# Unfolding products read PSUM, the first batch in a new block order with loads in halves, and a layout that knows the shared port

## The chip, the cores and the metric

One Trainium2 chip, one core of it. The metric is the device time of one execution in microseconds (us), median over several executions; lower is better. The engines are TensorE (PE; its weight loads are PEld), VectorE (DVE), ScalarE (ACT), GpSimd (POOL) and SyncE (SP), which issues all DMAs here.

## What is computed

Two stages over 8 batches, 8 heads, 576 positions, head size 64, all in float32. Stage 1 is attention in a sliding window; stage 2 takes its output as x and runs four small causal attentions ("experts") that a gate mixes, two per position.

```python
scores = scale * (q @ k.T)
mask = (rel >= 0) & (rel < 64)
attn = softmax(where(mask, scores, -1e9)) @ v
x = attn.transpose(0, 2, 1, 3).reshape(B, S, H * D)

logits = x @ w_gate
w = softmax of the two largest logits of a position
for e in range(4):
    q, k, v = x @ wq[e], x @ wk[e], x @ wv[e]
    a = softmax(where(causal, scale * (q @ k.T), -1e9))
    out += w[e] * (a @ v @ wo[e])
```

## The kernel before

The work is written as small functions and put in order by a planner. Class `Plan` records every engine call with a due time `at` and a cost; `order` is a list scheduler: on each engine it takes the ready operation with the smallest `at` whose buffers are free, and the calls are then issued in that order, which is fixed from there on. Waits on the chip come from data and buffers alone; each engine works its own queue from the front.

**Stage 1** works in 36 units `u` of 8 blocks. A block is 64 queries of one pair of heads `p` (four pairs make a batch, nine blocks a pair), so a batch is 36 blocks or 4.5 units, taken pair by pair.
- `s1_qk` (line 338): 32 small products into two PSUM banks `s1` (tag "s", 5 banks); ACT and DVE bring them to SBUF tile `sm`, folded, so that a row holds only the 64 scores of its window (ACT copies the earlier part, POOL writes it for a head's first block, DVE lays the own block over it); then DVE takes the row maximum, POOL subtracts it, ACT takes the exponential, DVE sums and inverts, POOL scales. The last lines load the next pair's q and k.
- `s1_t` (line 373): PE turns `sm` in four transposes into a PSUM bank `t1` (tag "t", 3 banks); ACT copies it to SBUF tile `f` (`ft`, 2 buffers); from `f` the folded rows are unfolded into `pt`: two triangle products on DVE (`pt<-ft,tri`) and two `affine_select` on POOL (`pt<-ft`).
- `s1_av` (line 393): 32 products with v into a bank `o1` (tag "t"); ACT writes the result rounded as `XH`, DVE the remainder as `XL`.

**Stage 2** of a batch takes `XH`, `XL` of all four pairs: `s2_v` (values and gate, four tiles of 128 positions and one tail), `proj` (`s2_k`, `s2_q`, columns in halves by `HALVES`), scores `s2_mm`, softmax `s2_soft`, `s2_t`, `s2_av_mm`, `s2_o`. The weights are loaded by `load_weight` and split into two parts by ACT and DVE (`split_weights`). Due times come from the tables `POS`, `BPOS` and `WPOS`.

Loads at the start, in SP's order: q and k of pair 0, of pair 1, v of pair 0, q and k of pair 2, v of pair 1, then weights, each tile whole; q, k and v have three buffers each, so pair p+3 is loaded where pair p is done with.

Of the kernel before, what the change touches and what calls it, by code (L numbers as in the profile page):

```python
# [8 lines left out]
F32 = mybir.dt.float32  # L9
# [18 lines left out]
FIXED = (1.0, 15.5)  # L28
WPOS = [-0.776, -0.284, -0.071, 1.269]
CPOS = 0.202  # L30
BPOS = ((0.044, 0.7), (0.088, 0.667), (0.08, 0.3, 0.12), (-0.413, -0.1))
PARTS = ((0, 5), (5, 9))
HALVES = ((0, 320), (320, 256))


class Plan:
# [64 lines left out]
    def link(self):  # L101
        seen, tiles = {}, {}
        for op in self.ops:
            deps, spare = {}, set()
            for x, w in op["use"]:
                if x.space not in (PSUM, bass.MemoryType.SB):
                    continue
                t = x.tensor.name
                box = self.box(x)
                bank = x.space == PSUM  # L110
                if t not in tiles:
                    tiles[t] = dict(first=op, ops=[], tag=x.tensor.tag, bufs=x.tensor.tag_meta.bufs, bank=bank)
                if not any(op is o for o in tiles[t]["ops"]):
                    tiles[t]["ops"].append(op)
                for other, b, ww in seen.setdefault(t, []):
                    if other is op:
                        continue
                    hit = box[0] < b[1] and b[0] < box[1] and box[2] < b[3] and b[2] < box[3]
                    if hit and (w or ww) or bank and other["engine"] != op["engine"]:
                        deps[other["n"]] = deps.get(other["n"], True) and (w and not bank)  # L120
                seen[t].append((op, box, w))
            op["deps"] = deps
        for t in tiles.values():
            t["left"] = len(t["ops"])
            for op in t["ops"]:
                op.setdefault("tiles", []).append(t)
        for t in tiles.values():
            first = t["first"]
            if t["bank"]:
                later = [o for o in t["ops"] if o["engine"] != "P"]  # L130
                for o in later:
                    for d, buffer_only in o["deps"].items():
                        if buffer_only and d < first["n"]:
                            first["deps"].setdefault(d, True)
                    for u in o["tiles"]:
                        if not u["bank"] and u["first"]["n"] > first["n"]:
                            u["first"] = first
                            for v in u["ops"]:
                                if v["n"] > first["n"]:
                                    v["deps"].setdefault(first["n"], True)  # L140
        for t in tiles.values():
            t["first"].setdefault("takes", []).append(t)
        return tiles

    def order(self):
# [16 lines left out]
        mode = None  # L162
        events = [0.0]
        ends = []
        done, now = [], 0.0
        while len(done) < len(ops):
# [18 lines left out]
            for e in "PAVGS":  # L185
# [25 lines left out]
                clock[e] = now + max(20, cost - self.OVERLAP[e])  # L211
# [7 lines left out]
        return done  # L219

    def place(self, op, mode):
        return op["at"]

    def issue(self):
        for op in self.order():
# [17 lines left out]
def window_attention_moe_attention(ctx: ExitStack, tc: tile.TileContext, qT, kT, vW,  # L243
# [9 lines left out]
    pairs = {}  # L253

    def load_pair(p):
        q_t = load.tile([128, S], F32, tag="q", bufs=3, name=f"q{p}")
        nc.sync.dma_start(q_t, qT[p])
        k_t = load.tile([128, S + 64], F32, tag="k", bufs=3, name=f"k{p}")
        nc.sync.dma_start(k_t, kT[p])
        pairs[p] = [q_t, k_t, None]  # L260

    def load_v(p):
        v_t = load.tile([128, 2, BLK, 64], F32, tag="v", bufs=3, name=f"v{p}")
        nc.sync.dma_start(v_t, vW[p].rearrange("r (h b c) -> r h b c", h=2, b=BLK))
        pairs[p][2] = v_t

# [4 lines left out]
    load_pair(0)  # L271
    load_pair(1)
    load_v(0)
    load_pair(2)
    load_v(1)


    own = const.tile([128, 64], mybir.dt.uint8, name="own")
# [51 lines left out]
    SM, PT1 = {}, {}  # L330
    XH, XL, XT = {}, {}, {}

    def tiles(u):
        for i in range(8):
            t = 8 * u + i
            yield i % 2, i // 2, t // BLK, t % BLK

    def s1_qk(u):

        banks = [psum.tile([128, 4, 128], F32, tag="s", bufs=5, name=f"s1_{u}_{x}") for x in range(2)]  # L340
        with nc.block():
            for x, j, p, b in tiles(u):
                c0 = 64 * int(b == 0)
                for h in range(2):
                    r, o = slice(64 * h, 64 * h + 64), 64 * (h ^ x)
                    nc.tensor.matmul(banks[x][o:o + 64, j, c0:], lhsT=pairs[p][0][r, 64 * b:64 * b + 64],
                                     rhs=pairs[p][1][r, 64 * b + c0:64 * b + 128], start=True, stop=True)
        sm = SM[u] = work.tile([128, 2, 4, 64], F32, tag="sm1", bufs=3, name=f"sm1_{u}")
        st = work.tile([128, 3, 8], F32, tag="st1", bufs=3, name=f"st1_{u}")
        first = {(x, j) for x, j, p, b in tiles(u) if b == 0}  # L350
# [9 lines left out]
            nc.vector.copy_predicated(sm[:, x], own[:, None, :].to_broadcast([128, 4, 64]), banks[x][:, :, 64:128])  # L360
        flat = sm.rearrange("r x j c -> r (x j) c")
        nc.vector.tensor_reduce(st[:, 0], flat, axis=AX.X, op=OP.max, negate=True)
        nc.gpsimd.tensor_tensor(flat, flat, st[:, 0, :, None].to_broadcast([128, 8, 64]), op=OP.add)
        nc.scalar.activation(flat, flat, AF.Exp, scale=0.125)
        nc.vector.tensor_reduce(st[:, 1], flat, axis=AX.X, op=OP.add)
        nc.vector.tensor_scalar_add(st[:, 1], st[:, 1], 1e-9)
        nc.vector.reciprocal(st[:, 2], st[:, 1])
        nc.gpsimd.tensor_tensor(flat, flat, st[:, 2, :, None].to_broadcast([128, 8, 64]), op=OP.mult)
        for x, j, p, b in tiles(u):
            if b == BLK - 1 and p + 3 < NB * NP:  # L370
                load_pair(p + 3)

    def s1_t(u):

# [3 lines left out]
            for i in range(4):  # L378
                nc.tensor.transpose(ps[:, i], sm[:, 128 * i:128 * i + 128], ident)
        t = PT1[u] = work.tile([128, 4, 2, 128], F32, tag="pt1", bufs=2, name=f"pt1_{u}")  # L380
        f = work.tile([128, 4, 128], F32, tag="ft", bufs=2, name=f"ft_{u}")
        nc.scalar.activation(f, ps, AF.Copy)
        for e in range(2):
            r = slice(64 * e, 64 * e + 64)
            nc.vector.tensor_mul(t[0:64, :, e], f[r],
                                 tri[r].rearrange("r a c -> r (a c)")[:, None, :].to_broadcast([64, 4, 128]))
            nc.gpsimd.affine_select(out=t[64:128, :, e].rearrange("r i (a c) -> r i a c", a=2),
                                    in_=f[r].rearrange("r i (a c) -> r i a c", a=2), pattern=[[0, 4], [0, 2], [1, 64]],
                                    base=0, channel_multiplier=-1, compare_op=OP.is_ge, fill=0.0)

    freed = []

    def s1_av(u):
# [11 lines left out]
        while i < 8:  # L405
            b9, k = divmod(8 * u + i, NP * BLK)
            n = min(8 - i, NP * BLK - k)
            if k == 0:
                XH[b9] = work.tile([128, NP * S], F32R, tag="xh", name=f"xh{b9}")
                XL[b9] = work.tile([128, NP * S], F32R, tag="xl", name=f"xl{b9}")  # L410
            c = slice(64 * k, 64 * (k + n))
            src = o[:, i:i + n].rearrange("r t c -> r (t c)")
            nc.scalar.activation(XH[b9][:, c], src, AF.Copy)
            nc.vector.tensor_sub(XL[b9][:, c], src, XH[b9][:, c])
            if k + n == NP * BLK:
                if b9 % 2 == 0:
                    for x in range(2):
# [5 lines left out]
        while freed and freed[0] + 3 in pairs:  # L423
            load_v(freed.pop(0) + 3)

# [119 lines left out]
                nc.vector.tensor_copy(G2[h][64:128, :, 7:9], src[64 * h:64 * h + 64, 0])  # L545

    def proj(b, name, pr, half):
        c0, n = HALVES[half]
# [194 lines left out]
    def s2_o(b, j):  # L743
        ps = psum.tile([128, DM], F32, tag="s", bufs=5, name=f"ops_{b}_{j}")
        with nc.block():
            for pr in range(2):
                y0 = y_col(b, 2 * j) if j < 4 else 512
                yh, yl = (y[pr][:, y0:y0 + 128] for y in (YH, YL))
                three(ps, yh, yl, whi["o"][:, pr], wlo["o"][:, pr], pr == 0, pr == 1)
        t = work.tile([128, DM], F32, tag="out", bufs=2, name=f"out_{b}_{j}")  # L750
        nc.vector.tensor_copy(t, ps)
        if j < 4:
            nc.sync.dma_start(out[b, 128 * j:128 * j + 128], t)
# [71 lines left out]
    todo.append((CPOS, stage2_constants, ()))  # L825
    todo.append((WPOS[2] + 1e-3, clear_pt2, ()))
    for i in range(4):
        load_weight(i)
        if i == 0:
            load_v(2)  # L830
    todo.sort(key=lambda x: x[0])
    for t, f, args in todo:
        nc.at = t
# [57 lines left out]
```

## Time and profile before

| | us |
|---|---|
| median of 3 runs | 513.28 (512.98 to 515.19) |
| profiled execution, its own time | 516.96 |
| its span, first to last instruction | 515.2 |
| TensorE busy | 476.6 (93%) |
| VectorE busy | 371.2 (72%) |
| ScalarE busy | 299.0 (58%) |
| GpSimd busy | 262.7 (51%) |
| DMA moved | 51.29 MB, mean 100 GB/s |

The profile is of one execution; its time is 3.7 us above the median of the runs. All rows name line 227, the planner's recording of a call, so groups are told by their tiles. [...]

### The profile page before, as it was taken

The numbers are of one execution on the slowest core, as the hardware profiler recorded it, in microseconds if no ns is written. First come the engines' busy times: TensorE is split into PE (matmuls) and PEld (weight loads), VectorE is DVE, ScalarE is ACT, GpSimd is POOL, SyncE is SP. The second block draws the span as 40 slices with busy tenths as digits, with TensorE's granted clock in tenths as the row PEclk, the third lists the DMA queues.
The fourth block names the chain that finished last, engine by engine and source line by source line (L and its number), as shares of the span: only waits on it lengthen the run. The fifth ranks groups of instructions, "written<-read, shape, count | busy, mean of one in ns | idle before, by whom it ended". The sixth has DMA issues, their size and how long they took to land.

```text
span 515.2 us, 14666 instructions
## 1 busy us (share of the span) xinstructions
PE 476.6 (93%) x5672; PEld 417.5 (81%) x5672; DVE 371.2 (72%) x1178; ACT 299.0 (58%) x929; POOL 262.7 (51%) x439
## 2 busy tenths in 40 slices
PE   4558989999999999999999999999999999999986
PEld 3447977888988888888888888888888888898774
DVE  5878778987676877878686777878677775644713
ACT  2534355766557475656657565665756575656651
POOL 5748727583566545383565536384465534422130
PEclk9966998999999999999999999999999999999979
DMA  8745432131552323241543223241341000201103
GB/s 297 292 124 197 136 115 78 68 95 48 186 156 77 98 87 96 74 135 46 160 155 103 73 91 116 63 146 46 115 147 60 1 22 22 63 1 43 42 1 103
DMA packets 20630, 51.29 MB, mean 100 GB/s; under 512 B 2768, under 2 KB 3280, under 8 KB 20560
## 3 DMA queue, kind: packets, MB, share of 16 engines
q1 hardware_dynamic: 20560, 50.35, 29.8%
q8 instruction: 45, 0.74, 0.6%
q14 instruction: 25, 0.20, 0.1%
HBM read 40.90 MB, written 9.44 MB: 98 GB/s over the span
## 4 chain that ended last, share of the span: by engine, by line
PE 66%; DVE 13%; POOL 12%; ACT 3%; issue 3%; DMA 1%; SPq 0%; POOLq 0%; DVEq 0%
PE s L227 14%; PE o L227 12%; PE t L227 11%; PE ops L227 10%; PE v2ps L227 8%; PE qps L227 7%; PE kps L227 5%; POOL p L227 5%; DVE st L227 4%; POOL sm L227 4%; POOL pt L227 3%; DVE g L227 2%; DVE p L227 1%; DMA k<-in_kT_dram 1%; DVE sm L227 1%
## 5 line engine op out<-in xcount | busy, mean ns | idle before, releaser
L227 POOL TENSOR_TENSOR sm<-sm,st 128x512 f32<-128x512 f32 x72 | 77.6, 1078 | 72.3 <-DVE st L227 52.7
L227 PE MATMUL o<-pt,v 128*64 128x64 f32 (+3 forms) x2048 | 95.3, 250 | 9.1 <-DVE pt L227 3.9
L227 PEld LDWEIGHTS o<-pt,v 128*64 128x64 f32 x2048 | 85.6, 144 | 20.1 <-POOL pt L227 9.5
L227 ACT ACTIVATE p<-p,r 128x192 f32<-128x192 f32 (+3 forms) x128 | 77.4, 607 | 31.9 <-DVE r L227 31.5
L227 POOL TENSOR_SCALAR_AFFINE_SELECT pt<-ft 64x512 f32<-64x512 f32 x72 | 64.4, 894 | 61.5 <-ACT ft L227 58.3
L227 POOL TENSOR_SCALAR p<-p,r 128x192 f32<-128x192 f32 (+3 forms) x128 | 77.9, 625 | 31.9 <-DVE r L227 14.8
L227 ACT ACTIVATE pt<-t 128x512 f32<-128x512 f32 (+2 forms) x192 | 69.5, 388 | 22.1 <-PE t L227 20.1
L227 DVE CUSTOM_DVE_ANT_0 p<-s,causal 128x320 f32<-128x320 f32 (+3 forms) x160 | 68.2, 470 | 7.1 <-PE s L227 6.6
L227 DVE TENSOR_TENSOR pt<-ft,tri 64x512 f32<-64x512 f32 x72 | 62.6, 869 | 4.8 <-ACT ft L227 3.5
L227 DVE TENSOR_REDUCE st<-sm 128x8 f32<-128x512 f32 x72 | 49.1, 684 | 17.0 <-ACT sm L227 15.8
L227 PE MATMUL t<-ident,p 128*128 128x128 f32 x384 | 59.2, 283 | 1.6 <-POOL p L227 1.5
L227 PE MATMUL s<-kt,qt 64*128 64x256 f32 (+2 forms) x480 | 55.0, 334 | 2.7 <-DVE sm L227 1.1
L227 PE MATMUL s<-k,q 64*64 64x128 f32 (+1 forms) x1152 | 45.5, 298 | 7.9 <-DMA k<-in_kT_dram 7.9
L227 PEld LDWEIGHTS t<-ident,p 128*128 128x128 f32 x384 | 44.3, 144 | 10.4 <-issue 2.7
L227 PEld LDWEIGHTS s<-k,q 64*64 64x64 f32 x1152 | 36.5, 151 | 14.7 <-issue 6.1
L227 DVE COPY_PREDICATED sm<-own,s 128x256 f32<-128x256 uint8 x72 | 30.5, 444 | 24.4 <-POOL sm L227 13.3
L227 PEld LDWEIGHTS s<-kt,qt 64*128 64x128 f32 x480 | 36.2, 185 | 13.0 <-issue 3.8
L227 PE MATMUL qps<-xh,wqhi 128*128 128x320 f32 (+1 forms) x128 | 40.7, 318 | 0.0
L227 PE MATMUL kps<-xh,wkhi 128*128 128x320 f32 (+1 forms) x128 | 39.6, 310 | 0.0
L227 ACT ACTIVATE sm<-sm 128x512 f32<-128x512 f32 x36 | 22.7, 630 | 28.2 <-POOL sm L227 27.8
L227 PE MATMUL v2ps<-wvhi,xh 128*128 128x260 f32 x128 | 38.8, 303 | 0.0
L227 PE MATMUL qps<-xl,wqhi 128*128 128x320 f32 (+1 forms) x128 | 37.8, 295 | 0.0
(105 smaller groups left out, 1044.3 us busy)
## 6 DMA issues: line engine op xcount, KB each, us to landing
v<-in_vW_dram SPq DMA_DIRECT2D x32, 576.0 KB, 4.1
k<-in_kT_dram SPq DMA_DIRECT2D x32, 320.0 KB, 3.9
q<-in_qT_dram SPq DMA_DIRECT2D x32, 288.0 KB, 3.0
out_dram<-out SPq DMA_DIRECT2D x32, 256.0 KB, 2.1
out_dram<-out SPq DMA_DIRECT2D x8, 128.0 KB, 2.3
pt<-in_wv_dram SPq DMA_DIRECT2D x1, 512.0 KB, 8.9
pt<-in_wk_dram SPq DMA_DIRECT2D x1, 512.0 KB, 8.8
pt<-in_wq_dram SPq DMA_DIRECT2D x1, 512.0 KB, 8.5
```

The lines of the kernel that those rows point to most:

```text
L227: call(*args, **kw)
```

## The change

1. Unfolding (`s1_t`): the triangle product reads the PSUM bank instead of the SBUF copy, in all units (`UNFOLD = (2, 2)`); POOL's selects still read the copy, which now has one buffer.
2. First batch: q and k of all four pairs are loaded, first columns 0 to 255, then the rest; `ORDER` takes blocks 0 to 3 of every pair first, then blocks 4 to 8; q, k and v have four buffers and k loses its 64 columns of zeros; `HALVES` of batch 0 is 256 and 320 columns. Units below `EARLY = 5` fold the subtraction of the maximum into eight exponentials of 64 columns with a bias, in place of POOL's subtraction. The splits into `XH`, `XL` follow the new block order.
3. Planner: operations that hold the port that VectorE and GpSimd share are charged for each other; all operations of a tile with several buffers wait for the tile's first one; due times of the weight loads; in the last batch the even output tiles take the buffers of `sm`. `AFFINITY = 0.0` changes nothing.

```diff
-HALVES = ((0, 320), (320, 256))
+HALVES = (((0, 256), (256, 320)), ((0, 320), (320, 256)))
...
+        sb = [x for x in outs + ins if x.space != PSUM]
+        op["port"] = engine == "G" or engine == "V" and (
+            len([x for x in sb if x in ins]) > 1 or len(sb) == len(outs + ins) and name in (
+                "tensor_copy", "tensor_scalar", "tensor_scalar_add"))
...
+                if best["port"]:
+                    cost += max(0.0, port - now)
+                    port = now + cost
...
-        q_t = load.tile([128, S], F32, tag="q", bufs=3, name=f"q{p}")
-        nc.sync.dma_start(q_t, qT[p])
-        k_t = load.tile([128, S + 64], F32, tag="k", bufs=3, name=f"k{p}")
-        nc.sync.dma_start(k_t, kT[p])
+        q_t = load.tile([128, S], F32, tag="q", bufs=4, name=f"q{p}")
+        k_t = load.tile([128, S], F32, tag="k", bufs=4, name=f"k{p}")
         pairs[p] = [q_t, k_t, None]
+        if p >= NP:
+            load_part(p, 0, S)
...
+    for p in range(NP):
+        load_part(p, 0, 256)
+    for p0 in (0, 2):
+        for p in (p0, p0 + 1):
+            load_part(p, 256, S)
+        for p in (p0, p0 + 1):
+            load_v(p)
...
+    ORDER = [(p, b) for p0 in (0, 2) for p in (p0, p0 + 1) for b in range(4)]
+    ORDER += [(p, b) for p in range(NP) for b in range(4, BLK)]
+    ORDER += [(p, b) for p in range(NP, NB * NP) for b in range(BLK)]
...
-        nc.gpsimd.tensor_tensor(flat, flat, st[:, 0, :, None].to_broadcast([128, 8, 64]), op=OP.add)
-        nc.scalar.activation(flat, flat, AF.Exp, scale=0.125)
+        if u < EARLY:
+            nc.vector.tensor_scalar(st[:, 0], st[:, 0], 0.125, None, op0=OP.mult)
+            for i in range(8):
+                nc.scalar.activation(flat[:, i], flat[:, i], AF.Exp, bias=st[:, 0, i:i + 1], scale=0.125)
+        else:
+            nc.gpsimd.tensor_tensor(flat, flat, st[:, 0, :, None].to_broadcast([128, 8, 64]), op=OP.add)
+            nc.scalar.activation(flat, flat, AF.Exp, scale=0.125)
...
-        f = work.tile([128, 4, 128], F32, tag="ft", bufs=2, name=f"ft_{u}")
+        f = work.tile([128, 4, 128], F32, tag="ft", bufs=1, name=f"ft_{u}")
         nc.scalar.activation(f, ps, AF.Copy)
...
-            nc.vector.tensor_mul(t[0:64, :, e], f[r],
-                                 tri[r].rearrange("r a c -> r (a c)")[:, None, :].to_broadcast([64, 4, 128]))
+            if e < UNFOLD[u >= EARLY]:
+                nc.vector.tensor_mul(t[0:64, :, e], ps[r],
+                                     tri[r].rearrange("r a c -> r (a c)")[:, None, :].to_broadcast([64, 4, 128]))
...
+        tag, bufs = ("out", 2) if b < NB - 1 or j % 2 else ("sm1", 3)
...
+        nc.at = (-99.0, -1.7, -1.7, -0.9)[i]
         load_weight(i)
```

The instructions move most in front of the first dense work of stage 2, the values product `v2ps_0` of batch 0. On TensorE, before (s is `s1_qk` of the unit named first, t its transposes, o its products with v; k_161 is a tile of batch 1's pairs), the rows that lead up to it:

```order
L227 MATMUL s_7_0_192<-k_148,q_147 64x128 x2
L227 MATMUL s_7_1_193<-k_161,q_160 64x64 x2
L227 MATMUL o_4_162<-pt_4_154,v_128 64x64 x8
L227 MATMUL o_4_162<-pt_4_154,v_139 64x64 x8
L227 MATMUL t_5_170<-ident,sm_5_158 128x128 x4
L227 MATMUL v2ps_0_183<-wvhi,xh_116 128x260
```

and in the change:

```order
L241 MATMUL s_4_1_146<-k_78,q_77 64x128 x2
L241 MATMUL s_4_0_145<-k_127,q_126 64x64 x2
L241 MATMUL s_4_1_146<-k_127,q_126 64x128 x2
L241 MATMUL s_4_0_145<-k_127,q_126 64x128 x2
L241 MATMUL s_4_1_146<-k_127,q_126 64x128 x2
L241 MATMUL t_3_142<-ident,sm_3_134 128x128 x4
L241 MATMUL v2ps_0_186<-wvhi,xh_117 128x260
```

Before, units 0 to 7 of s, 0 to 5 of t and 0 to 4 of o stand ahead of `v2ps_0`; now 0 to 4 of s, 0 to 3 of t and 0 to 2 of o.

On VectorE, the unfolding of unit 0 (`st` is the row statistics), before:

```order
L227 TENSOR_REDUCE st_2_124<-sm_2_123 128x8
L227 TENSOR_TENSOR pt_0_107<-ft_108,tri 64x4x128 x2
L227 TENSOR_TENSOR pt_1_119<-ft_120,tri 64x4x128 x2
L227 TENSOR_REDUCE st_2_124<-sm_2_123 128x8
L227 TENSOR_SCALAR st_2_124<-st_2_124 128x8
```

and in the change:

```order
L241 TENSOR_SCALAR st_2_125<-st_2_125 128x8
L241 TENSOR_TENSOR pt_0_110<-t_0_109,tri 64x4x128
L241 TENSOR_REDUCE st_1_115<-sm_1_114 128x8
L241 TENSOR_TENSOR pt_0_110<-t_0_109,tri 64x4x128
L241 TENSOR_SCALAR st_1_115<-st_1_115 128x8
L241 TENSOR_REDUCE st_2_125<-sm_2_124 128x8
```

The products read the bank `t_0` and have a reduction of the next unit between them.

## Rows read from the trace of the kernel before

**Rows 1.** Windows: start, all between, end (PE, PEld, DVE, ACT, POOL busy; clock; DMA)
```profile
0.00:80.00 80.00, 56.61 (x765) 49.09 (x765) 61.47 (x141) 35.16 (x92) 48.06 (x95) 0.89 0.55 187
80.00:480.00 400.00, 391.76 (x4677) 345.81 (x4678) 296.51 (x992) 246.72 (x786) 208.39 (x334) 1.00 0.27 86
480.00:515.20 35.20, 28.25 (x232) 22.60 (x230) 13.22 (x48) 17.11 (x52) 6.28 (x11) 0.90 0.15 53
```
**Rows 2.** Waits of TensorE from 0 to 50 us: total us, times, longest
```profile
PE t L227 <- POOL sm L227: 6.8, 5, 3.1
```
**Rows 3.** Timeline of TensorE, 0 to 62 us: start, length, operation
```profile
4.66 2.19 PE L227 MATMUL s<-k,q 64*64 64x64 f32 x36 [4.66 <-DMA k<-in_kT_dram]
...
14.21 1.12 PE L227 MATMUL t<-ident,sm 128*128 128x128 f32 x4 [1.80 <-POOL sm L227]
...
39.97 1.11 PE L227 MATMUL t<-ident,sm 128*128 128x128 f32 x4 [3.10 <-POOL sm L227]
...
44.69 2.39 PE L227 MATMUL o<-pt,v 128*64 128x64 f32 x32
47.01 1.39 PE L227 MATMUL s<-k,q 64*64 64x128 f32 x32
48.32 1.15 PE L227 MATMUL o<-pt,v 128*64 128x64 f32 x32
49.41 0.65 PE L227 MATMUL t<-ident,sm 128*128 128x128 f32 x4
49.81 0.37 PE L227 MATMUL v2ps<-wvhi,xh 128*128 128x260 f32 x1
```
**Rows 4.** Timeline of VectorE, 0 to 42 us
```profile
6.89 0.77 DVE L227 COPY_PREDICATED sm<-own,s 128x256 f32<-128x256 uint8 x2 [2.76 <-ACT sm L227]
...
15.99 4.26 DVE L227 TENSOR_TENSOR pt<-ft,tri 64x512 f32<-64x512 f32 x4
```
**Rows 5.** Tile ft: every use, duration in ns as least/median/most
```profile
L227 DVE TENSOR_TENSOR pt<-ft,tri x72: 672/720/1424, 16.0 to 424.6; 64x512 f32<-64x512 f32 x72
L227 POOL TENSOR_SCALAR_AFFINE_SELECT pt<-ft x72: 661/996/2134, 16.1 to 428.9; 64x512 f32<-64x512 f32 x72
L227 ACT ACTIVATE ft<-t x36: 570/592/600, 15.4 to 423.2; 128x512 f32<-128x512 f32 x36
```
**Rows 6.** Groups by form: busy us, mean ns of one | idle before
```profile
L227 POOL TENSOR_TENSOR sm<-sm,st 128x512 f32<-128x512 f32 x72 | 77.6, 1078 | 72.3 <-DVE st L227 52.7 <-ACT sm L227 5.7 <-DVE gs L227 4.3
...
L227 DVE TENSOR_REDUCE st<-sm 128x8 f32<-128x512 f32 x72 | 49.1, 684 | 17.0 <-ACT sm L227 15.8
...
L227 DVE TENSOR_TENSOR xl<-o,xh 128x512 fp32r<-128x512 f32 x32 | 21.8, 681 | 2.8 <-ACT xh L227 2.5
...
L227 DVE RECIPROCAL st<-st 128x8 f32<-128x8 f32 x36 | 7.2, 199 | 0.5
...
L227 ACT ACTIVATE px<-px,r 128x64 f32<-128x64 f32 x16 | 5.3, 333 | 0.0
```
**Rows 7.** Line 227 on ScalarE, 13 to 14 us: duration ns least/median/most
```profile
L227 ACT ACTIVATE sm<-s x3: 205/268/385, 13.3 to 13.5; 128x64 f32<-128x64 f32 x1, 128x128 f32<-128x128 f32 x1, 128x256 f32<-128x256 f32 x1
```
**Rows 8.** Timeline of ScalarE: these three together
```profile
13.27 0.65 ACT L227 ACTIVATE sm<-s 128x64 f32<-128x64 f32 x3
```
**Rows 9.** Windows: clock and DMA rate in two stretches
```profile
10.00:15.00 5.00, 2.51 (x30) 1.91 (x28) 4.40 (x11) 1.88 (x6) 2.50 (x4) 1.00 1.07 392
...
38.00:40.00 2.00, 0.03 (x1) 0.03 (x1) 1.50 (x5) 1.18 (x4) 1.59 (x3) 0.50 0.95 356
```
**Rows 10.** Timeline of SP: DMA issues, first and fourth
```profile
0.80 0.40 SPq L227 DMA_DIRECT2D q<-in_qT_dram  x1
...
2.19 0.43 SPq L227 DMA_DIRECT2D k<-in_kT_dram  x1
```
**Rows 11.** Chain that ended last: end of unit 2's o, one key product
```profile
29.32 1.55 PE o L227 x24
...
51.52 1.75 PE kps L227 x12
```

More of the change, by code (lines that the diff above doesn't have):

```diff
@@ L30 @@
 CPOS = 0.202
+EARLY = 5
+AFFINITY = 0.0
+UNFOLD = (2, 2)
 BPOS = ((0.044, 0.7), (0.088, 0.667), (0.08, 0.3, 0.12), (-0.413, -0.1))
 PARTS = ((0, 5), (5, 9))
-HALVES = ((0, 320), (320, 256))
+HALVES = (((0, 256), (256, 320)), ((0, 320), (320, 256)))
 class Plan:
@@ L142, in link @@
             t["first"].setdefault("takes", []).append(t)
+            if t["bufs"] > 1:
+                for o in t["ops"]:
+                    if o is not t["first"]:
+                        o["deps"].setdefault(t["first"]["n"], False)
         return tiles
@@ L161, in order @@
         clock = {e: 0.0 for e in "VAGPS"}
-        mode = None
+        mode, port = None, 0.0
         events = [0.0]
@@ L210, in order @@
                 best["start"] = now
-                clock[e] = now + max(20, cost - self.OVERLAP[e])
+                clock[e] = best["pend"] = now + max(20, cost - self.OVERLAP[e])
                 end = now + cost + {"P": 200, "S": 2000}.get(e, 0)
@@ L221, in place @@
     def place(self, op, mode):
-        return op["at"]
+        return op["at"] - (AFFINITY if op["mode"] == mode is not None else 0)
     def issue(self):
@@ L255, in load_pair, with load_part @@
     def load_pair(p):
-        q_t = load.tile([128, S], F32, tag="q", bufs=3, name=f"q{p}")
-        nc.sync.dma_start(q_t, qT[p])
-        k_t = load.tile([128, S + 64], F32, tag="k", bufs=3, name=f"k{p}")
-        nc.sync.dma_start(k_t, kT[p])
+        q_t = load.tile([128, S], F32, tag="q", bufs=4, name=f"q{p}")
+        k_t = load.tile([128, S], F32, tag="k", bufs=4, name=f"k{p}")
         pairs[p] = [q_t, k_t, None]
+        if p >= NP:
+            load_part(p, 0, S)
+    def load_part(p, c0, c1):
+        nc.sync.dma_start(pairs[p][0][:, c0:c1], qT[p][:, c0:c1])
+        nc.sync.dma_start(pairs[p][1][:, c0:c1], kT[p][:, 64 + c0:64 + c1])
     def load_v(p):
-        v_t = load.tile([128, 2, BLK, 64], F32, tag="v", bufs=3, name=f"v{p}")
+        v_t = load.tile([128, 2, BLK, 64], F32, tag="v", bufs=4, name=f"v{p}")
         nc.sync.dma_start(v_t, vW[p].rearrange("r (h b c) -> r h b c", h=2, b=BLK))
@@ L270, in window_attention_moe_attention @@
     PX = [const.tile([128, 2, 64], F32, name="px")]
[L271 to L275, printed above, removed]
+    for p in range(NP):
+        load_pair(p)
+    for p in range(NP):
+        load_part(p, 0, 256)
[4 more added lines that the diff above has]
+            load_v(p)
     own = const.tile([128, 64], mybir.dt.uint8, name="own")
@@ L346, in s1_qk @@
                     nc.tensor.matmul(banks[x][o:o + 64, j, c0:], lhsT=pairs[p][0][r, 64 * b:64 * b + 64],
-                                     rhs=pairs[p][1][r, 64 * b + c0:64 * b + 128], start=True, stop=True)
+                                     rhs=pairs[p][1][r, 64 * b + c0 - 64:64 * b + 64], start=True, stop=True)
         sm = SM[u] = work.tile([128, 2, 4, 64], F32, tag="sm1", bufs=3, name=f"sm1_{u}")
@@ L369, in s1_qk @@
         for x, j, p, b in tiles(u):
-            if b == BLK - 1 and p + 3 < NB * NP:
-                load_pair(p + 3)
+            if b == BLK - 1 and p + NP < NB * NP:
+                load_pair(p + NP)
     def s1_t(u):
@@ L384, in s1_t @@
             r = slice(64 * e, 64 * e + 64)
-            nc.vector.tensor_mul(t[0:64, :, e], f[r],
-                                 tri[r].rearrange("r a c -> r (a c)")[:, None, :].to_broadcast([64, 4, 128]))
-            nc.gpsimd.affine_select(out=t[64:128, :, e].rearrange("r i (a c) -> r i a c", a=2),
-                                    in_=f[r].rearrange("r i (a c) -> r i a c", a=2), pattern=[[0, 4], [0, 2], [1, 64]],
-                                    base=0, channel_multiplier=-1, compare_op=OP.is_ge, fill=0.0)
+            if e < UNFOLD[u >= EARLY]:
+                nc.vector.tensor_mul(t[0:64, :, e], ps[r],
+                                     tri[r].rearrange("r a c -> r (a c)")[:, None, :].to_broadcast([64, 4, 128]))
+            for half in range(e < UNFOLD[u >= EARLY], 2):
+                nc.gpsimd.affine_select(out=t[64 * half:64 * half + 64, :, e].rearrange("r i (a c) -> r i a c", a=2),
+                                        in_=f[r].rearrange("r i (a c) -> r i a c", a=2), pattern=[[0, 4], [0, 2], [2 * half - 1, 64]],
+                                        base=half - 1, channel_multiplier=1 - 2 * half, compare_op=OP.is_ge, fill=0.0)
     freed = []
@@ L410, in s1_av @@
                 XL[b9] = work.tile([128, NP * S], F32R, tag="xl", name=f"xl{b9}")
[L411 to L414, printed above, removed]
+            at = [S * (p % NP) + 64 * b for p, b in ORDER[8 * u + i:8 * u + i + n]]
+            j = 0
+            while j < n:
+                m = next((m for m in range(1, n - j) if at[j + m] != at[j] + 64 * m), n - j)
+                w = 1
+                while at[j + w * m:j + w * m + m] == [x + S * w for x in at[j:j + m]]:
+                    w += 1
+                yh, yl = (y[b9].rearrange("r (p c) -> r p c", p=NP)[:, at[j] // S:at[j] // S + w, at[j] % S:at[j] % S + 64 * m]
+                          if w > 1 else y[b9][:, at[j]:at[j] + 64 * m] for y in (XH, XL))
+                src = o[:, i + j:i + j + w * m].rearrange("r t c -> r (t c)")
+                if w > 1:
+                    src = src.rearrange("r (p c) -> r p c", p=w)
+                nc.scalar.activation(yh, src, AF.Copy)
+                nc.vector.tensor_sub(yl, src, yh)
+                j += w * m
             if k + n == NP * BLK:
@@ L422, in s1_av @@
             i += n
-        while freed and freed[0] + 3 in pairs:
-            load_v(freed.pop(0) + 3)
+        while freed and freed[0] + NP in pairs:
+            load_v(freed.pop(0) + NP)
     PT2 = [const.tile([128, 2, 576 if part == 0 else 1024], F32, name=f"pt2_{part}") for part in range(2)]
@@ L547, in proj @@
     def proj(b, name, pr, half):
-        c0, n = HALVES[half]
+        c0, n = HALVES[b > 0][half]
         ps = psum.tile([128, 512], F32, tag="s", bufs=5, name=f"{name}ps_{b}_{pr}_{half}")
@@ L749, in s2_o @@
                 three(ps, yh, yl, whi["o"][:, pr], wlo["o"][:, pr], pr == 0, pr == 1)
-        t = work.tile([128, DM], F32, tag="out", bufs=2, name=f"out_{b}_{j}")
+        tag, bufs = ("out", 2) if b < NB - 1 or j % 2 else ("sm1", 3)
+        t = work.tile([128, DM], F32, tag=tag, bufs=bufs, name=f"out_{b}_{j}")
         nc.vector.tensor_copy(t, ps)
```

5 lines of the change are left out of this document (1 added, 4 removed).

## The prediction

> **What bounds the kernel now.** I read three stretches first. TensorE is idle for 23.4 us of the first 80 (80 less 56.61), 8.2 us of the next 400 and 7.0 us of the last 35.2 [rows 1]. From 80 us on it is 98% busy, and the change leaves it the same products; so what there is to win lies in the first 50 us. There the waits of TensorE name the softmax of stage 1: its transposes wait 6.8 us for the scaled scores on POOL [rows 2]. The timeline of TensorE shows why: unit 0's products come at 4.66 us, its transposes only at 14.21, and dense work, in which one product follows the other, begins at 49.81 with the first values product of batch 0 [rows 3]. I call that point M. On VectorE the four triangle products of units 0 and 1 take 4.26 us together, where one that is undisturbed takes 0.67 [rows 4, 5]: POOL's selects, which read the same copy, take turns with them, and reach 2.1 us where an undisturbed one takes 0.66 [rows 5].
>
> The clock has to be read with care. The windows row from 10 to 15 us says 1.00, yet the four transposes at 14.21 take 1.12 us, as they do at 39.97 (1.11) where the row says 0.50, and not 0.65 as at 49.41 [rows 3, 9]. So I price TensorE's early work at half rate. [...] By the clock row M below would come about 2.5 us earlier and the time would be 500.8.
>
> **The change, part by part.** I follow the new order to M and then compare what is left to do.
>
> *Loads.* Issues on SP follow each other at 0.47 us (0.80 to 2.19 for the first four) [rows 10]. Unit 0 now needs four tiles of 128 KB, all issued by 2.2 us, instead of 608 KB; unit 0's products then end at about 5.4 us instead of 6.6 (4.66 and 32 of 36 products in 2.19) [rows 3]. All of q, k and v for four pairs, 4.7 MB, stand ahead of the first weights; at 392 GB/s [rows 9] that is 12 us, and the first 608 KB, 1.6 us of it, were there at 4.66, so it lasts until about 15.1; the weights, 2 us of issues and pair 4's q and k follow by about 20. They are needed first behind unit 1's result, at 24 us, so I cost them at nothing; the cover is 4 us, and each us beyond it would delay M by one. On SP the load of pair 4 waits for unit 2's products and has the key and query weights behind it; those products are due at 11 us.
>
> *Softmax of an early unit.* POOL's subtraction (1.08 us [rows 6]) and one exponential go; a small product on DVE and eight exponentials of 64 columns come. Nothing like these eight is in the trace. Three copies of 205, 268 and 385 ns took 0.65 us together [rows 7, 8], so one behind another costs about 0.1 us more: eight would take 0.9 us. An exponential of 64 columns with an accumulator takes 0.333 [rows 6], eight of them 2.7. I take 1.2, near the copies, for nothing is accumulated. The way from the first own-block copy to the transposes is then 0.77 + 0.68 + 0.2 + 1.2 + 0.68 + 0.4 + 1.08 = 5.0 us [rows 4, 6] and, by my estimate, 0.1 for each of eight handovers: 5.8. From 5.7 (the copy at 6.89 came 0.3 behind its products) the transposes of unit 0 start at 11.5, before 14.21.
> [...]
>
> *Unfolding.* A triangle product that reads PSUM and one SBUF tile is not in the trace; the nearest, the remainder `xl` of 512 columns, takes 0.68 us [rows 6], so I take 0.68, between the undisturbed 0.67 and today's median of 0.72 [rows 5]. With one SBUF operand I expect no turns with POOL, so selects go to 0.66. Unit 0: transposes to 12.6; DVE product, reduction, product 2.1 us, to 14.7; ACT copy 0.6 and two selects 1.3 to 14.6. Its products with v start at 14.8; today DVE's four end at 20.3 [rows 4].
> The single `ft` buffer adds a wait: unit 2's copy waits for unit 1's selects, and behind it on ACT stand four exponentials of unit 3.
>
> *To M.* At half rate: o of unit 0 (2.39) to 17.2, s of unit 3 (1.95) to 19.2, transposes of 1 and 2 (2 x 1.1) to 21.4 [rows 3]. Copy, selects, second copy, selects follow one another to 24.4. With o of units 1 and 2, s of unit 4 and t of unit 3 at full rate (1.15, 1.15, 1.39, 0.65 [rows 3]) M is at 27.7; at half rate at 30.3. Unit 3's own softmax, from 19.5 and 5.8 long, shares DVE with six operations of 0.68 and is ready by 25.3 to 29.4. I take 29.0 for M. Below, DVE has 17.4 us of work from 5.7 to the split of the value weights, without a gap to 23.1: M no earlier than 24. Above: in today's trace unit 2's o ended at 30.9 [rows 11], and unit 4's s and unit 3's t at half rate, with a wait as today's longest before a transpose (3.1), make about 36.
>
> *Behind M.* Three s, two t and two o less stand ahead of M: 3 x 1.39 + 2 x 0.65 + 2 x 1.15 = 7.8 us, done later. Then comes a stretch in which DVE has more to do than TensorE. Up to the second key product of batch 0: four values products of 260 columns and four key and query products of 256, by width from the 1.75 of 320, one of 320, three s, two o, two t: 20.8 us [rows 3, 11]. DVE: eight own-block copies 3.1, eight reductions 5.5, six triangle products 4.1, three weight splits of 1024 columns 3.6, seven pieces of `xl` 2.7 (three more than before), five remainders of k and q 2.0, fourteen small ones 2.8: 23.8 us. (The prices by width are an estimate from the 0.68 us of 512 columns, 0.15 of it to start.) So TensorE waits 3.0 us there.
>
> *The rest.* DVE and POOL get back some 0.2 us an operation later on; that work lies beside TensorE, so I count nothing. Four load buffers, the output tiles in `sm`'s buffers and the port in the planner move little of TensorE's order behind the first batch: nothing. The last 7 us of idle stay.
>
> **Sum.** 49.8 - 29.0 - 7.8 - 3.0 = 10.0 us less. Against the profiled execution: 516.96 - 10.0 = 507.0. That execution is 3.7 us above the median; from 513.28 the forecast is **503.3 us**. With M at 24 it is 498.3, with M at 36 510.3.
>
> **The rivals.**
> *VectorE paces the start.* If DVE keeps the share that it holds today once it has begun (some 80%: 61.47 of 80 us, less 3 of the first 7) [rows 1], its 41.2 us from 5.7 to that second key product last until 57.2 instead of 52.8. The gain is 5.6 and the time 507.7. For it: its in-order queue waits for four engines. Against: some of today's share is turns with POOL that go away.
> *Slower: the PSUM banks of tag "t" are held.* Today ACT's copy (0.59) frees a transposes' bank; now it also waits for two triangle products with a reduction between them in DVE's queue, 2.0 us, and the copy for the only `ft`. Three banks serve t and o of both stages. If that makes TensorE wait 0.32 us in each of the 31 later units the gain is gone, from 0.41 the kernel is slower; with 1.4 us in every second unit, 21.7 us, it takes 525.0. For it: DVE's queue is full. Against: from 80 us on TensorE is idle 8.2 us in all, 0.27 a unit, so the banks are not short now.
> *The early order brings nothing.* If the weights come later than 24 us by more than the cover, because pair 4's load holds SP up, M slips by as much; 10 us late, the time is 513.3.
>
> **Chances.** The forecast 0.62, VectorE as pace 0.20, nothing won 0.08, held banks 0.10. A measurement of this kernel can tell about 0.5%, 2.6 us, from no change. So faster by more than that 0.82, within it 0.08, slower 0.10. The range, from the bounds of M and with VectorE's case inside, is 498.0 to 510.5.
>
> **What would show it.** Right: the first values product at 26 to 33 us; unit 0's transposes near 11.5; idle of TensorE in the first 80 us down to about 13; triangle products with a median of 0.68 and no case near 1.4; selects near 0.66. Wrong: M behind 36 us, waits of the first values product for a weight, idle of TensorE in the 400 us behind the start well over 8 us with waits before t or o, or eight exponentials that take over 2.5 us.

## The result and the profile after

The change takes 493.75 us (median of 4 runs, 493.07 to 494.5) beside 513.54 for the kernel before on the same chip: a ratio of 0.961, interval 0.958 to 0.964. That is 19.8 us less where 10.0 was forecast, and below the forecast range (498.0 to 510.5). The profiled execution took 494.5 us, its span is 492.8.

Windows of the change, to be read beside [rows 1] (behind the engines' busy times stand TensorE's granted clock, 1.00 at full rate, the DMA share and GB/s); the last stretch is shorter by what the span lost:
```profile
0.00:80.00 80.00, 61.85 (x870) 53.78 (x871) 63.48 (x168) 45.90 (x139) 43.04 (x100) 0.94 0.64 212
80.00:480.00 400.00, 396.46 (x4742) 351.70 (x4741) 288.45 (x1012) 262.25 (x824) 188.45 (x335) 1.00 0.25 80
480.00:492.80 12.80, 8.11 (x64) 6.30 (x62) 4.04 (x7) 1.37 (x5) 0.00 (x0) 0.97 0.31 104
```
Idle of TensorE falls in the first 80 us from 23.4 to 18.2, and in the next 400 us from 8.2 to 3.5, the part that was forecast to stay. The stage-1 units of the middle show it in the waits of TensorE from 130 to 400 us, the kernel before first (total us, times, longest):
```profile
PE t L227 <- POOL sm L227: 2.8, 4, 0.8
PE o L227 <- POOL pt L227: 1.4, 2, 0.7
PE s L227 <- DVE logits L227: 1.0, 3, 0.3
PE s L227 <- DVE m L227: 0.6, 2, 0.3
```
and all that the change has there:
```profile
PE s L241 <- DVE logits L241: 0.4, 1, 0.4
```
TensorE's timeline of the start, which answers to [rows 3]:
```profile
13.30 1.11 PE L241 MATMUL t<-ident,sm 128*128 128x128 f32 x4 [2.14 <-DVE st L241]
16.00 0.70 PE L241 MATMUL o<-pt,v 128*64 128x64 f32 x8 [1.58 <-POOL pt L241]
17.46 1.55 PE L241 MATMUL o<-pt,v 128*64 128x64 f32 x24 [0.76 <-DVE pt L241]
...
31.68 0.37 PE L241 MATMUL v2ps<-wvhi,xh 128*128 128x260 f32 x1
...
138.36 0.37 PE L241 MATMUL v2ps<-wvhi,xh 128*128 128x260 f32 x1
```
The last two rows are the first values product of batch 0 (point M) and of batch 2. The same product of batch 2 in the kernel before:
```profile
148.85 0.37 PE L227 MATMUL v2ps<-wvhi,xh 128*128 128x260 f32 x1
```
By the lead I mean how much earlier the change starts the same product than the kernel before. It is 18.1 us at batch 0 and 10.5 at batch 2, near the 10.0 of the sum. But it then grows, by 5 us every two batches, to 20.2 at batch 6. The stretch from batch 2 to batch 6, in the kernel before and in the change:
```profile
148.85:383.94 235.09, 229.57 (x2837) 201.97 (x2838) 181.21 (x583) 145.16 (x463) 127.81 (x201) 1.00 0.33 105
138.36:363.70 225.34, 225.34 (x2838) 200.58 (x2838) 174.12 (x583) 148.90 (x463) 113.90 (x200) 1.00 0.33 105
```
The products are the same but for one at the edge, and the granted clock reads 1.00 in both. TensorE's idle falls from 5.5 us to nothing, and its busy time by 4.2 us.

The triangle products of the change, by tile `t` (ns least/median/most), beside [rows 5]:
```profile
L241 DVE TENSOR_TENSOR pt<-t,tri x72: 669/688/695, 15.2 to 401.9; 64x512 f32<-64x512 f32 x72
```
POOL's selects, by tile `ft`:
```profile
L241 POOL TENSOR_SCALAR_AFFINE_SELECT pt<-ft x72: 660/663/1222, 15.3 to 402.1; 64x512 f32<-64x512 f32 x72
```
The eight exponentials of unit 0, ScalarE's timeline:
```profile
8.48 2.01 ACT L241 ACTIVATE sm<-sm,st 128x64 f32<-128x64 f32 x8
```
A triangle product that reads the bank has no slow case left: 695 ns at most, where the copy cost up to 1424. In b_unfold below, where the operand alone differs from the kernel before, it is 694. The selects fall from a median of 996 ns to 663, and the longest from 2134 to 1222. "Port" and "turns" stand for these durations; which other operations of VectorE and GpSimd slow each other is the author's assumption in the planner, which no run tests by itself.

The product still waits for ACT's copy of the same bank. In unit 0, on VectorE and on ScalarE:
```profile
15.19 0.68 DVE L241 TENSOR_TENSOR pt<-t,tri 64x512 f32<-64x512 f32 x1 [0.63 <-ACT ft L241]
15.90 0.69 DVE L241 TENSOR_REDUCE st<-sm 128x8 f32<-128x512 f32 x1
16.62 0.69 DVE L241 TENSOR_TENSOR pt<-t,tri 64x512 f32<-64x512 f32 x1
```
```profile
14.58 0.57 ACT L241 ACTIVATE ft<-t 128x512 f32<-128x512 f32 x1
```
In the traces of the kernel before, of the change and of b_unfold below, the first product of each of the 36 units starts behind the end of its copy (by 32 ns or more in the first two). So the new operand takes away the product's turns with POOL, and not the wait for the copy.

### The profile page after: what moved, and what is told of

Same layout as the page of the kernel before. It is cut to its first block, busy times and chain, and to the rows that moved or that the text cites. A ratio compares the mean times of both kernels' runs of the same rounds, so it can differ in the third digit from the quotient of the medians.

```text
span 492.8 us, 14724 instructions
## 1 busy us (share of the span) xinstructions
PE 466.4 (95%) x5672; PEld 411.8 (84%) x5672; DVE 356.0 (72%) x1186; ACT 309.5 (63%) x967; POOL 231.5 (47%) x434
## 4 chain that ended last, share of the span: by engine, by line
PE 86%; DVE 6%; ACT 4%; issue 1%; POOL 1%; DMA 1%; SPq 1%; POOLq 0%; ACTq 0%
PE s L241 17%; PE o L241 17%; PE t L241 13%; PE ops L241 11%; PE qps L241 10%; PE v2ps L241 10%; PE kps L241 10%; ACT sm L241 2%; DVE st L241 2%; DVE pt L241 2%; DMA k<-in_kT_dram 1%; DVE sm L241 1%; ACT p L241 1%; SPq L241 1%; DVE p L241 0%
## 5 line engine op out<-in xcount | busy, mean ns | idle before, releaser
L241 POOL TENSOR_TENSOR sm<-sm,st 128x512 f32<-128x512 f32 x67 | 71.5, 1070 | 86.4 <-DVE st L241 53.6
L241 PE MATMUL o<-pt,v 128*64 128x64 f32 (+3 forms) x2048 | 94.3, 248 | 6.7 <-DVE pt L241 3.5
L241 POOL TENSOR_SCALAR p<-p,r 128x192 f32<-128x192 f32 (+3 forms) x128 | 72.7, 587 | 38.7 <-DVE r L241 24.0
L241 ACT ACTIVATE pt<-t 128x512 f32<-128x512 f32 (+2 forms) x192 | 69.8, 386 | 15.9 <-PE t L241 13.8
L241 DVE CUSTOM_DVE_ANT_0 p<-s,causal 128x320 f32<-128x320 f32 (+3 forms) x160 | 70.5, 471 | 11.5 <-PE s L241 10.3
L241 POOL TENSOR_SCALAR_AFFINE_SELECT pt<-ft 64x512 f32<-64x512 f32 x72 | 48.3, 671 | 54.8 <-ACT ft L241 50.7
L241 DVE TENSOR_TENSOR pt<-t,tri 64x512 f32<-64x512 f32 x72 | 49.4, 686 | 6.4 <-ACT ft L241 5.3
L241 PE MATMUL s<-kt,qt 64*128 64x256 f32 (+2 forms) x480 | 53.2, 336 | 0.4 <-DVE logits L241 0.4
L241 PEld LDWEIGHTS s<-k,q 64*64 64x64 f32 x1152 | 35.5, 147 | 12.9 <-issue 4.7
L241 PEld LDWEIGHTS s<-kt,qt 64*128 64x128 f32 x480 | 34.9, 186 | 10.6 <-issue 4.1
L241 PE MATMUL kps<-xh,wklo 128*128 128x320 f32 (+1 forms) x128 | 37.6, 294 | 0.0
```

The source lines that it names most:

```text
L241: call(*args, **kw)
```

## The experiments

Three parts are told apart: **U**, products read PSUM; **S**, the new first batch (block order, halves, four buffers, eight exponentials); **P**, the planner's two rules. What else the change does (one `ft` buffer, due times of the weight loads, output tiles in the buffers of `sm`) stays in every run with S and goes with it. Every run was timed beside the kernel before, whose median was 514.4 to 514.7 us in these sessions.

### Each part alone, and the operand at a fixed order

*b_unfold*: the kernel before with U alone; the order of every engine's instructions stays as it was.
```diff
-            nc.vector.tensor_mul(t[0:64, :, e], f[r],
+            nc.vector.tensor_mul(t[0:64, :, e], ps[r],
```


> The kernel before with one edit: the triangle products read the PSUM bank in place of the SBUF copy; every engine's order of instructions stays as it was. Theory P (turns at the shared port cost TensorE time all through the kernel): products fall from a mean of 0.87 us to 0.69, selects from 0.89 to 0.67, and the kernel is faster by 8 to 14 us (500 to 505.5), most of it won between 130 and 420 us. Theory O (the gain behind the start comes from the planner's new order): products and selects get shorter too, but the kernel gains under 3 us (510.5 to 513.5).

Measured: 504.54 us, ratio 0.978 (0.973 to 0.983), as theory P said. Products fall from a mean of 0.87 us to 0.69 and selects from 0.89 to 0.69. So 10 us come from the operand alone, with no instruction moved.

*a_start*: the change with U and P undone, S alone left.
```diff
-            if t["bufs"] > 1:
+            if False:
...
-                if best["port"]:
+                if False:
...
-                nc.vector.tensor_mul(t[0:64, :, e], ps[r],
+                nc.vector.tensor_mul(t[0:64, :, e], f[r],
```


> The changed kernel without its first and third part: products read the SBUF copy, the planner has neither the port nor the new rule on tiles with several buffers. What is left is the first batch (block order, loads in halves, eight exponentials) with four load buffers and one ft buffer. Theory P: the start alone, 5 to 9 us faster than before (504.5 to 508.5), since the turns at the port eat into it. Theory O: 8 to 11 us faster (502.5 to 505.5), and the planner would bring the rest.

Measured: 521.08 us, ratio 1.012 (1.007 to 1.016): slower, and outside what either theory said. Its batch 0 starts 16 us early and batch 2 late:
```profile
33.95 0.57 PE L241 MATMUL v2ps<-wvhi,xh 128*128 128x260 f32 x1
...
154.76 0.37 PE L241 MATMUL v2ps<-wvhi,xh 128*128 128x260 f32 x1
```
In between TensorE waits for VectorE and POOL (its waits from 60 to 140 us):
```profile
PE t L241 <- POOL sm L241: 3.4, 2, 2.9
PE s L241 <- DVE r L241: 3.0, 1, 3.0
PE s L241 <- DVE kt L241: 1.5, 1, 1.5
PE qps L241 <- DVE m L241: 1.3, 1, 1.3
PE o L241 <- DVE gs L241: 1.2, 1, 1.2
```

*x_psum* and *x_sbuf*: the change, planned as if the products waited for bank and copy both, so that one order serves either operand; the second reads the copy.
```diff
+                nc.ops[-1]["use"].append((f[r], False))
```
```diff
+                call, args, kw = nc.ops[-1]["calls"][-1]
+                nc.ops[-1]["calls"][-1] = (call, (args[0], f[r], *args[2:]), kw)
```


> The changed kernel, planned as if the triangle products needed both the bank and the SBUF copy; they read the bank. It is the partner of x_sbuf, which has the same order of instructions. Both theories: within 3 us of the changed kernel (491 to 497).

> The same order of instructions as x_psum, but the triangle products read the SBUF copy. Theory P: 8 to 16 us slower than x_psum, products and selects back near 0.87 and 0.89 us. Theory O: within 3 us of x_psum.

Measured: 491.5 us (0.954, 0.949 to 0.959) and 498.91 (0.968, 0.964 to 0.972): the operand is worth 7.4 us in the same order, a little under theory P's 8 to 16. (x_psum is 2 us below the change, though the intervals touch; its planner charges the wait for the copy, which the products do have.) But x_sbuf, without U, is still nearly 16 us faster than the kernel before, which S cannot have brought. That left the planner.

### Is it the planner?

*a_plan* (U and S, both rules off), *a_noport* (only the port rule off), *b_plan* (P alone on the kernel before), *b_uplan* (U and P). The edits are `if False:` at the two conditions as above, or these lines put into the kernel before:
```diff
+            if t["bufs"] > 1:
+                for o in t["ops"]:
+                    if o is not t["first"]:
+                        o["deps"].setdefault(t["first"]["n"], False)
...
+                if best["port"]:
+                    cost += max(0.0, port - now)
+                    port = now + cost
```


> The change without the two new rules of the planner (first instruction of a tile first; turns at the shared port); the unfolding from PSUM and the new first batch stay. Theory G: the start's 10 us are kept because VectorE and POOL no longer take turns at the port: 493 to 498 us, TensorE's lead over the kernel before at equal work not shrinking between 50 and 135 us. Theory R: the planner's rules keep them, and the two parts only add up: 521.1 (new first batch alone) less the 10 that the unfolding alone won, 508 to 513 us, with a lead that falls from 10 to about 3 by 135 us.

> The change without the port rule alone; the rule on a tile's first instruction stays. Theory G: as the change, 493 to 498 us. Theory R: if the port rule is what keeps the lead, 505 to 513 us; if it is the rule on a tile's first instruction, 493 to 496 us here and over 505 in the run without both.

> The kernel before with the two planner rules alone: products still read the SBUF copy, old first batch. Theory G: the order alone wins little while the turns at the port stay: 511 to 515 us. Theory R: the rules are worth 5 to 10 us by themselves: 503 to 508 us.

> The kernel before with the unfolding from PSUM and both planner rules, old first batch. Theory G: as the unfolding alone, 503 to 506 us; the rest up to the change, 10 us, is then the new first batch. Theory R: 494 to 499 us, and the new first batch is worth less than 5 us.

Measured: a_plan 500.44 us (0.973, 0.970 to 0.976), a_noport 498.47 (0.969, 0.966 to 0.971), b_plan 499.93 (0.971, 0.968 to 0.974), b_uplan 497.46 (0.966, 0.963 to 0.968). Theory G falls: the rules alone bring 14.6 us, with products that still read the copy. Of theory R's numbers only b_uplan's held (a_plan is 8 us below its range): U and P do not add up.

*b_port* and *b_first*: one rule each on the kernel before.

> The kernel before with the port rule in the planner alone (an instruction that uses the shared port is planned to wait for the one before it there); products read the SBUF copy. Theory T (the planner believed too early ends on VectorE and POOL, so it put transposes and products of stage 1 too early into TensorE's order; charging the turns moves them back): most of the two rules' 14.6 us, 500 to 504 us. Theory F (the rule on a tile's first instruction does it, by ordering the instructions that share a tile): 511 to 515 us.

> The kernel before with the rule on a tile's first instruction alone. Theory T: 510 to 515 us. Theory F: 499 to 504 us. If the two runs share the gain, 505 to 509 us in each.

Measured: b_port 501.97 us (0.977, 0.974 to 0.979), b_first 518.78 (1.010, 1.006 to 1.013). It is the port rule, as theory T said. The other rule alone does harm, more than either theory allowed; beside U and S it may help (a_plan less a_noport, 2.0 us; the intervals touch). How the port rule works shows in the written order. One place on TensorE in the kernel before, with the transposes of unit 30, and the same transposes with the port rule:
```
1735 L227 MATMUL t_4_1_0_1_813<-ident,p_0_67 128x128 x4
1736 L227 MATMUL t_30_816<-ident,sm_30_800 128x128 x4
1737 L227 MATMUL kps_1_0_819<-xh_615,wkhi 128x320
```
```
1754 L234 MATMUL o_4_1_0_824<-pt_0_83,v_0_97 64x96 x2
1755 L234 MATMUL t_30_816<-ident,sm_30_800 128x128 x4
1756 L234 MATMUL s_5_0_0_0_825<-kt_0_806,qt_87 128x256
```
The transposes now stand behind those key products and two groups of products with v. The trace of the kernel before has this place (four transposes of `p`, then those of `sm`, then the key products), and the wait in it:
```profile
354.30 0.66 PE L227 MATMUL t<-ident,sm 128*128 128x128 f32 x4 [0.76 <-POOL sm L227]
```
On average over units 8 to 35, 19,200 columns of other products stand between a unit's last score product and its first transpose before, 19,000 with the first-instruction rule, 23,900 with the port rule. The traces show the same in time. In the kernel before, POOL's last work on a unit's `sm` ends 10.2 us behind the last score product of that unit (mean of these units), and its transposes start 11.3 us behind it; in b_port these are 11.5 and 13.0 us, in b_unfold 9.4 and 10.9, in b_first 10.5 and 11.2. The planner had left the transposes too little room: 1.1 us on average between the two, where it is 1.5 with the port rule or with U and 0.7 with the first-instruction rule. In b_port the waits from 130 to 400 us shrink to one row, while its selects stay slow (median 998 ns, as before), so this is a later place in TensorE's queue and not a faster POOL. (The rule moves instructions on VectorE and POOL too; what that does by itself no run shows.) Its waits of TensorE:
```profile
PE kps L234 <- DVE logits L234: 0.2, 1, 0.2
```
and its selects, by tile `ft`:
```profile
L234 POOL TENSOR_SCALAR_AFFINE_SELECT pt<-ft x72: 660/998/1217, 15.8 to 414.4; 64x512 f32<-64x512 f32 x72
```
In b_first, the waits of TensorE in the same stretch grow:
```profile
PE t L231 <- POOL sm L231: 8.1, 7, 1.8
```

### What the new first batch needs, and the eight exponentials

*a_sbuf*: the change without U, planned anew (the edit of the product's operand as in a_start). *a_early0* and *a_early1*: `EARLY = 0` and `EARLY = 1`. *x_early0*: x_psum with `EARLY = 0`.

> The change with the products reading the SBUF copy again, planned anew; both planner rules and the new first batch stay. Theory A (the planner's rules took most of the time out, and the unfolding from PSUM removes the same waits a second time): 495 to 498 us, that is 499.9 of the two rules alone less the 3.7 that the new first batch won on top of rules and unfolding. Theory B (the new first batch needs the unfolding to keep its lead, as it did without the rules): 500 to 506 us.

> The change without the eight exponentials for the first five units (EARLY 0: POOL subtracts the maximum and one exponential of 512 columns follows, in every unit). The eight took 2.01 us in unit 0 where 1.2 was forecast; subtraction and one exponential take 1.08 and 0.63 in the kernel before. If the eight bring the start forward by sparing POOL and its handover, this run is slower by 1 to 4 us, 495 to 498 us, and unit 0's transposes start behind 13.3 us. If they bring nothing, 492 to 495 us, with transposes at 13.3 or before.

> The change with the eight exponentials in unit 0 alone (EARLY 1). If the cost of the eight sits in units 1 to 4, where they stand on ACT in front of copies that VectorE waits for, this run is as the one without them, 487 to 490 us, with the first values product at 26 to 28 us. If it sits in unit 0, whose eight took 2.01 us, 492 to 495 us, with that product at 30 to 32 us.

> A version meant to beat both: the change without the eight exponentials, planned as if the products waited for the SBUF copy as well (worth 2 us before). If the two add up, 486 to 488 us; if the first already had what the second brought, 488 to 491 us.

Measured: a_sbuf 502.94 us (0.977, 0.971 to 0.983). Theory B holds: without U the new first batch does not pay, with the rules as without them, although its point M is 5 us earlier than in the change:
```profile
26.85 0.48 PE L241 MATMUL v2ps<-wvhi,xh 128*128 128x260 f32 x1
...
140.83 0.37 PE L241 MATMUL v2ps<-wvhi,xh 128*128 128x260 f32 x1
```
a_early0 takes 488.99 us (0.951, 0.947 to 0.956), below both of its forecasts and the lowest median of the study (though the intervals of x_psum, a_early1 and x_early0 overlap with its own); the eight exponentials cost the change some 5 us. Two rows of its TensorE timeline, with one exponential in every unit:
```profile
13.71 1.11 PE L241 MATMUL t<-ident,sm 128*128 128x128 f32 x4 [1.84 <-POOL sm L241]
...
26.60 0.37 PE L241 MATMUL v2ps<-wvhi,xh 128*128 128x260 f32 x1
```
Unit 0's transposes come 0.4 us later than with the eight and M 5 us earlier. Part of these 5 us is the clock. The granted clock of a stretch before M, in the change, in a_early1 and in a_early0:
```profile
24.40:31.10 6.70, 5.45 (x88) 4.91 (x88) 4.78 (x9) 3.82 (x10) 3.40 (x6) 0.50 0.40 134
```
```profile
26.10:31.00 4.90, 3.92 (x63) 3.35 (x59) 3.58 (x7) 1.90 (x6) 2.46 (x4) 0.50 0.39 122
```
```profile
18.00:26.60 8.60, 5.97 (x132) 4.86 (x129) 8.19 (x14) 5.78 (x11) 6.05 (x10) 1.00 0.96 353
```
In the change and in a_early1 TensorE ran at the half rate there, in a_early0 at the full. Half of the change's 5.45 us of busy time, an estimated 2.7 us, is what that can cost. No run shows whether the fall comes from the order or differs from one execution to the next. a_early1 takes 490.49 (0.953, 0.949 to 0.956), between its two forecasts. By the time it cannot be told from a_early0 and is clear of the change (0.958 to 0.964), so most of the cost lies in units 1 to 4. M in its trace, at 31.39, is where the other case had it, but it was reached at the lower clock and does not decide. x_early0 takes 490.12 (0.952, 0.947 to 0.957): the two improvements do not add up.

### All combinations

The medians, and in the traces the start of the first values product of batches 0, 2 and 6, with the lead over the kernel before in brackets:

| parts | us | batch 0 | batch 2 | batch 6 |
|---|---|---|---|---|
| none | 514.5 | 49.81 | 148.85 | 383.94 |
| U (b_unfold) | 504.54 | 46.97 (2.8) | 143.13 (5.7) | 372.26 (11.7) |
| P (b_plan) | 499.93 | 42.29 (7.5) | 140.64 (8.2) | 368.67 (15.3) |
| U, P (b_uplan) | 497.46 | 47.03 (2.8) | 141.18 (7.7) | 367.47 (16.5) |
| S (a_start) | 521.08 | 33.95 (15.9) | 154.76 (-5.9) | 389.89 (-5.9) |
| S, P (a_sbuf) | 502.94 | 26.85 (23.0) | 140.83 (8.0) | 370.44 (13.5) |
| S, U (a_plan) | 500.44 | 31.76 (18.1) | 139.05 (9.8) | 368.19 (15.8) |
| S, U, P (the change) | 493.75 | 31.68 (18.1) | 138.36 (10.5) | 363.70 (20.2) |

The starts come from one profiled execution each, and these lie up to 2.6 us from the medians (the kernel before took 516.96, b_unfold 501.9), so a lead can be off by some us: at the end of the span U's is 15.1, where the medians give 10.0. From batch 2 to batch 6 the granted clock reads 1.00 in all eight traces, so how the leads grow there is not the clock.

U and P have each a lead that grows from batch 2 to batch 6 (by 6.0 and 7.1 us), with both by 8.8 to 9.7: they take out the same waits, one by making VectorE and POOL ready earlier, the other by having TensorE come later. S has a lead that does not grow. It is worth -6.6 us alone, -3.0 beside P, +4.1 beside U and +3.7 beside both. The two gains are medians of different sessions; by the ratios they are 2.8 and 2.4 us, and the intervals overlap, so that they are gains is likely and not shown.

## Why the prediction was wrong

- **The step that failed is "The rest"**, and the premise behind it, that "what there is to win lies in the first 50 us": the relief of DVE and POOL "lies beside TensorE, so I count nothing", and the port in the planner moves "little of TensorE's order behind the first batch: nothing". U alone is worth 10.0 us and the port rule alone 12.5 (514.5 less 501.97), most of it behind batch 0: 8.9 of U's 11.7 us of lead at batch 6 come after batch 0's first values product, and 10.0 of the port rule's 14.1 (b_port's trace). The change gains 9.7 us between batches 2 and 6, which is what the forecast lacks.
- What misled me was one figure: 8.2 us of idle in 400. It is right, but I took it for what must stay, and the waits hide more than that. Of the 9.7 us between batches 2 and 6, 5.5 were idle in plain sight. The other 4.2 were counted as busy, for the same products at a clock of 1.00 in both kernels. Single products last as long in both (the 64 `v2ps<-wvhi,xl` 285 ns on average, the 640 `o` products of 64 columns 226 and 225), so what goes is short delays between their starts, which the modelled ends of products cover. Over the whole span TensorE's busy time fell by 10.2 us (476.6 to 466.4) for 5672 products. The mean granted clock rose from 0.974 to 0.985; with 0.50 as the lower level, the lowest that the windows rows show, that is an estimated 26.8 us and 14.8 us at half rate (2 x 0.026 x 515.2 and 2 x 0.015 x 492.8), so by this column at most some 6 us of the 10.2 are the clock, and none of it from batch 2 to batch 6.
- **The start**: forecast M 29.0, measured 31.68; transposes of unit 0 forecast 11.5, measured 13.30; its products with v 14.8, measured 16.00 and, for most of them, 17.46. The mis-sized term is the eight exponentials, 1.2 us forecast and 2.01 measured, 0.8 of the 1.8 us by which the transposes are late; the first own-block copy came 0.5 us late (6.18 for 5.7), and on VectorE two such copies of unit 1 stand in unit 0's way. Behind the transposes the forecast let VectorE's products run beside ACT's copy; they wait for it, and the second ends at 17.31 where 14.7 was forecast. The row of the three copies was the wrong neighbour for a biased activation: one of these eight lasts 337 ns on average, near the 333 of the exponential with an accumulator [rows 6], where the copy of 64 columns took 205 [rows 7]; the overlap between neighbours is an estimated 0.1 us in both ((8 x 0.337 - 2.01) / 7, and (0.858 - 0.65) / 2 for the copies). The 0.1 us for each handover rested on no row; behind the exponentials the change shows 0.03 (10.49 to 10.52, ScalarE to VectorE) and 0.15 (12.06 to 12.21, VectorE to POOL).
- **Behind M**: forecast 10.8 us given back between M and the dense part; measured, from the lead at batch 0 to that at batch 2, 7.6 in the change, but 21.8 in a_start and 15.0 in a_sbuf. VectorE's shortage there was named with the right sign; that it depends on the unfolding was not. The 0.15 us to start in its prices by width had no row; the `xl` remainders of 512 and 256 columns, 681 and 409 ns on average in the kernel before, give an estimated 0.14.
- That the start's sum of 10.0 matches the lead of 10.5 at batch 2 is in part chance: M came 2.7 us later than forecast and 3.2 us less were given back behind it, two errors that cancel. S by itself brings 3.7 us beside U and P, and U and P hold 7.7 us of lead at batch 2 without it.
- **Right**: products at 0.688 (0.68 forecast), selects at 0.663 (0.66); faster by more than 0.5%. The rival "banks held" did not occur: the waits before t and o in the middle went away. What "VectorE paces the start" feared, more given back behind M, came in a_start and a_sbuf, not in the change. **Missed** beside the times: idle of TensorE in the first 80 us, 18.2 where about 13 was forecast.

## What to carry to other kernels

Where an engine that looks saturated runs a fixed order, price a change to its neighbours by what it does to the waits in that order, and don't price it at nothing because the engine's idle share is small: here 2% of idle went with a gain of nearly 4%. In a static planner a wrong cost is a change of order, and charging the turns of two engines there was worth as much (12.5 us) as taking them away on the chip (10.0). Make a table of the parts in all combinations before crediting one: the new first batch alone was slower, and if it paid, it did so only beside the unfolding.

## What the runs showed that I had not expected

- An earlier M says little of the end: a_sbuf reached M 4.8 us before the change and ended 9.2 us behind it.
- In a_early0 the mean granted clock goes with the time: its four executions had spans of 490.0, 488.1, 486.4 and 484.6 us at clocks of 0.982, 0.992, 0.996 and 0.997. It is no rule: executions of the kernel before had spans of 512.4 us at 0.972 and 513.2 at 0.986. In a_early0's trace TensorE is at full rate from the transposes at 18.63 on (8 in 1.23 us, where 4 took 1.11 at 13.71). In the change's it reaches full rate in the transposes at 20.85 and loses it again: from 24.64 its products take twice as long (32 of unit 4's scores 1.96 us at 29.37, where a_early0 has 32 in 1.10 at 23.02). Both idled shortly before, the change 1.64 us and a_early0 1.58, so that does not tell them apart. The rows of the change:
```profile
20.85 1.12 PE L241 MATMUL t<-ident,sm 128*128 128x128 f32 x8
23.61 0.45 PE L241 MATMUL o<-pt,v 128*64 128x64 f32 x8 [1.64 <-POOL pt L241]
24.64 2.27 PE L241 MATMUL o<-pt,v 128*64 128x64 f32 x32 [0.58 <-DVE pt L241]
...
29.37 1.96 PE L241 MATMUL s<-k,q 64*64 64x128 f32 x32
```
- The windows row of a_early0 says 1.00 at 10 to 15 us, while four transposes take 1.11 us and not 0.65: as in the kernel before, where 1.11 us goes with a row of 0.50 [rows 3, 9], I read the early clock from the durations and not from that column. The row:
```profile
10.00:15.00 5.00, 2.41 (x20) 1.71 (x24) 4.08 (x10) 1.54 (x4) 3.09 (x3) 1.00 1.00 363
```
and the first transposes at full rate in its timeline:
```profile
18.63 1.23 PE L241 MATMUL t<-ident,sm 128*128 128x128 f32 x8
```
